# Seven block products instead of eight in the second MLP of a fused SSD, SwiGLU and softplus kernel

## The chip, the cores and the metric

The kernel runs on one core of a Trainium2 chip. The metric is the device time of one execution in microseconds (us), and what counts is the median of several executions. The profile is of one further execution on the same kind of core, and its times are counted from the start of its span. Engine names are those of the profile: PE is TensorE's matmuls, PEld its weight loads, DVE is VectorE, ACT is ScalarE, POOL is GpSimd, SP the engine that issues most DMAs.

## The reference

Three stages follow one another: a chunked state-space scan per head, a SwiGLU MLP, and an MLP with softplus. All is in fp32.

```python
# x: (4, 8, 768, 32); a: (4, 8, 768); B, C: (4, 8, 768, 16)
y = scan(x, a, B, C)                      # state carried along the 768 positions, per batch and head
x = y.transpose(0, 2, 1, 3).reshape(3072, 256)
xn = x / sqrt(mean(x * x, -1) + 1e-6) * rms_g
x = (silu(xn @ w_gate) * (xn @ w_val)) @ w_out        # layer 1: 256 -> 1536 -> 256
g = softplus(x @ w_in)                                # layer 2, first product: 256 -> 2048
return g @ w_out2                                     # layer 2, second product: 2048 -> 256
```

## The kernel before

The 3072 tokens are worked on as 24 units of 128 tokens (one batch, 128 positions). Four units make a tile of 512 tokens, so there are six tiles, 0 to 5. Tile t holds positions 128t to 128t+127 of all four batches, so the scan's state goes from each unit to the unit of the next tile with the same batch.

Both MLP layers keep features on the 128 partitions and 512 tokens along the free axis. Every product of two fp32 matrices is made of three fp32r matmuls: each operand is split into a high part and a rest, and high x high, rest x high and high x rest are added up in PSUM (`three_pass`, L834). One such matmul has a 128x128 weight and 512 columns.

- Layer 1 of a tile has 12 feature blocks f. `front1` (L857) makes gate and value of a block with 6 matmuls each into two banks of PSUM (tag `p`, 4 banks), ACT applies silu, DVE multiplies, `split_h` (L846) splits the result (ACT copies the high part, L396, DVE subtracts, L403) into a buffer `hw` (two of them). `back` (L891) multiplies it by `w_out` with 6 matmuls, adding to two banks of tag `t`. That is 18 matmuls a block, 216 a tile.
- Layer 2 of a tile has 16 blocks. `front2` (L877) makes 6 matmuls with `w_in` (names `wih`, `wil`), ACT applies softplus (L885), `split_h` splits, `back` makes 6 matmuls with the second weight (`wph`, `wpl`). That is 12 a block, 192 a tile, 96 of them in the first product.
- At the end of layer 1 the two `t` banks are split into `xxh` and `xxl`, the input of layer 2 (L927). At the end of layer 2 they are copied to buffers `s` (three of them, which softplus uses too) and sent to the output (L935).

The scan of a unit (`unit`, L533) needs two DVE scans (L604), two products with the decay (L653) and many small matmuls into banks of tag `a` (two). After four units, `norm` (L735) computes the RMS norm of the tile (L748 is its first operation on DVE for tiles 2 to 5, the split of the normalised input at L403 its last). `split` (L518) prepares B and C of a tile through buffers `wr` (three), through which the 34 chunks of weights come too (`weight`, L464).

What runs when is decided by a planner (`Plan`, L78 to L321) that writes out an order for every engine before the kernel is built. Each operation has a rank, a nominal time. The order of the layers is the list `seq` (L448 to L450): layer 1 of tiles 0 and 1, layer 2 of 0 and 1, then layer 1 and layer 2 of tile 2, of tile 3, then layer 1 of tiles 4 and 5, then layer 2 of 4 and 5. The planner starts an operation when its engine and its inputs are free, the lowest rank first; buffers of one tag are given out strictly in the order of the rank of their first operation (L189). The ranks of the scan (`base_of`, L511) and of `split` hang on the nominal start of layer 1 of their tile. Where layer 2 follows layer 1 of the same tile, two blocks of the next tile's layer 1 (`EARLY`) are put in between.

Of the kernel before, what the change touches and what calls it, by code (L numbers as in the profile page):

```python
# [17 lines left out]
P = 128  # L18
# [10 lines left out]

PAIRS = 2  # L30

EARLY, HEAD, TAIL = 2, 2, 2

FILL, SPARE = 200, 1e6

# [292 lines left out]
def tile_ssd_then_swiglu_then_softplus_mlp(  # L328
# [106 lines left out]
    W = {}  # L435
# [10 lines left out]
    blk_of = [i for i, b in enumerate(blocks) for _ in range(b["nu"])]  # L446

    seq = [(1, t) for t in range(HEAD)] + [(2, t) for t in range(HEAD)]  # L448
    seq += [(layer, t) for t in range(HEAD, len(blocks) - TAIL) for layer in (1, 2)]
    seq += [(layer, t) for layer in (1, 2) for t in range(len(blocks) - TAIL, len(blocks))]  # L450
    for layer, t in seq:
        b = blocks[t]
        b[f"t{layer}"] = t_nom
        t_nom += F1 * b["d1"] + b["nu"] * 1.4 if layer == 1 else F2 * b["d2"] + b["nu"] * 1.4


    chunks = []
# [385 lines left out]
    def wkeys(wt, f):  # L843
        return [(wt, f // 2, 0), (wt, f // 2, 1)]

    def split_h(key, s, n, rank, early=False):  # L846
        if early:
            hhl = buf("wr", [P, 8 * P + 64], I32, N_W)
            hhl.view = lambda t: t[:, 0:8 * P].bitcast(F32R).rearrange("p (s i) -> p s i", s=2)
        else:  # L850
            hhl = buf("hw", [P, 2, 4 * P], F32R, N_H)
        sv = lambda: s()[:, 0:n]
        COPY(n, rank - EPI, lambda: hhl()[:, 0, 0:n], sv, [s], [hhl])
        REST(n, rank - EPI, lambda: hhl()[:, 1, 0:n], sv, lambda: hhl()[:, 0, 0:n], [s, hhl], [(hhl, 1)], ("dve",))
        H[key] = hhl

    def front1(t, f, rank, new_table, early=False):  # L857
        bl = blocks[t]
        n = bl["n"]
        xh, xl = xnT[t]  # L860
        xk = xkeys[t]
        ps = []
        for wt in ("wg", "wv"):
            gp = pbuf("p", [P, 4 * P])
            PE(6 * n * MM * 1e3, rank, lambda gp=gp, wt=wt: three_pass(gp()[:, 0:n], wt, f, xh(), xl(), n),
               xk + wkeys(wt, f), [gp], 6 * n)
            ps.append(gp)
        s = buf("s", [P, 4 * P], F32, N_S)
        ACT(n, rank - EPI, lambda: act.activation(out=s()[:, 0:n], in_=ps[0]()[:, 0:n], func=ACTF.Silu), [ps[0]],  # L869
            [s, "table"] if new_table else [s], 1283 if new_table else 0)  # L870
        if not new_table:
            plan.readers.setdefault("table", []).append(len(plan.ops) - 1)
        DVE(n, rank - EPI, lambda: dve.tensor_tensor(out=s()[:, 0:n], in0=s()[:, 0:n], in1=ps[1]()[:, 0:n], op=ALU.mult),  # L873
            [s, ps[1]], [s], port=False)
        split_h((1, t, f), s, n, rank, early)

    def front2(t, f, rank, new_table):  # L877
        bl = blocks[t]
# [9 lines left out]
            plan.readers.setdefault("table", []).append(len(plan.ops) - 1)  # L888
        split_h((2, t, f), s, n, rank)

    def back(layer, t, f, rank):  # L891
        bl = blocks[t]
        n = bl["n"]
        nf, wt = ((F1, "wo"), (F2, "wp"))[layer - 1]
        if f == 0:
            acc[t] = [pbuf("t", [P, 4 * P]) for _ in range(KD)]
        hhl = H.pop((layer, t, f))

        end = (layer, t) == seq[-1] and f == nf - 1
# [12 lines left out]
        for m in range(0 if end else KD):  # L912
            def prod(m=m, o=acc[t][m]):
                a, b = (W[wt][s][:, f, m] for s in (0, 1))
                mm(o()[:, 0:n], a, swap(hhl()[:, 0, 0:n]), f == 0, False)
                mm(o()[:, 0:n], a, swap(hhl()[:, 1, 0:n]), False, False)
                mm(o()[:, 0:n], b, swap(hhl()[:, 0, 0:n]), False, f == nf - 1)
            PE(3 * n * MM * 1e3, rank, prod, [hhl, (hhl, 1)] + wkeys(wt, f), [acc[t][m]], 3 * n)
        if f < nf - 1:
            return  # L920
        if layer == 1:
            x2[t] = [buf(f"xx{k}", [P, KD, 4 * P], F32R, 3) for k in "hl"]
            for m in range(KD):
                h, l = ((lambda s=s, m=m: x2[t][s]()[:, m, 0:n]) for s in (0, 1))
                av = lambda a=acc[t][m]: a()[:, 0:n]
                COPY(n, rank - EPI, h, av, [acc[t][m]], [(x2[t][0], m)], False)
                DVE(n, rank - EPI, lambda h=h, l=l, av=av: dve.tensor_tensor(out=l(), in0=av(), in1=f32(h()), op=ALU.subtract),  # L927
                    [acc[t][m], (x2[t][0], m)], [(x2[t][1], m)], port=False)
        else:
            for m in range(KD):  # L930
                o = buf("s", [P, 4 * P], F32, N_S)
                COPY(n, rank - EPI, lambda o=o: o()[:, 0:n], lambda a=acc[t][m]: a()[:, 0:n], [acc[t][m]], [o], False,
                     ("dve",) if end and m else ("act",))
                c0 = bl["u0"] * P
                plan.op({"actq" if end and m else "sp": (1024, lambda o=o, m=m, q=act if end and m else nc.sync: q.dma_start(  # L935
                    out=out[m, :, c0:c0 + n], in_=o()[:, 0:n]))}, rank, [], [o])

    with tc.manual_schedule():
        plan.now = LOADS - 10
# [88 lines left out]
                steps = []  # L1028
        for c in range(len(chunks)):
            weight(c)  # L1030
        done = set()
        for j, (layer, t) in enumerate(seq):
            bl = blocks[t]
            if layer == 1:
                new = True
                for f in range(F1):
                    if (t, f) not in done:
                        front1(t, f, bl["t1"] + f * bl["d1"], new and j > 0 and seq[j - 1][0] == 2)
                        new = False
# [12 lines left out]


# [62 lines left out]
```

## Time and profile before

| | us |
|---|---|
| median of 3 executions (601.42 to 602.54) | 601.43 |
| the profiled execution | 600.79 |
| its span | 598.9 |
| PE busy | 593.7 (99%) |
| PEld busy | 513.3 (86%) |
| DVE busy | 351.3 (59%) |
| ACT busy | 310.0 (52%) |

The rows further down come from these views. The page's first part gives busy times, and its second the span in 40 slices. The view of waits says which engine stood idle for whom. The chain of work is followed back from the last instruction. The groups of instructions give how long one takes. The windows give the busy time of each engine in a stretch, and the timeline single instructions in order of time. The duration of a matmul in the profile overlaps that of the next: how fast matmuls follow one another is read from a run of them in the chain. Operations of DVE overlap in their records too.

### The profile page before, as it was taken

The page shows a single profiled execution, that of the slowest core. Times are in us where ns is not written, and L with a number is a line of the kernel's source. Part 1 is how long each engine was busy: PE and PEld are TensorE (multiplying, and loading weights), DVE is VectorE, ACT ScalarE, POOL GpSimd, SP SyncE. Part 2 cuts the span into 40 slices and gives each one's busy share as a digit, 9 for nine tenths or more (in the row PEclk, how much of TensorE's full clock was granted, in tenths as well). Part 3 has the DMA queues.
Part 4 walks back from the last instruction along what each step waited for, and adds up shares of the span by engine and source line. Part 5 has one row for each costly group of instructions (what it writes and reads, how often), then busy time and mean ns, then how long its engine had stood idle before and what let it go on. Part 6 is the DMA issues. An engine that isn't in the chain of part 4 may idle for free.

```text
span 598.9 us, 8785 instructions
## 1 busy us (share of the span) xinstructions
PE 593.7 (99%) x3385; PEld 513.3 (86%) x3385; DVE 351.3 (59%) x561; ACT 310.0 (52%) x547; POOL 19.7 (3%) x41
## 2 busy tenths in 40 slices
PE   9999999999999999999999999999999999999997
PEld 7888888888888888888888888888888888888886
DVE  6899978598876236694433779755333433322222
ACT  2676754678775445454555345655433333644543
POOL 3300000000000000000000000000000000000000
PEclk9999999999999999999999999999999999999999
DMA  6566648475661014111346433300000000000000
GB/s 213 189 223 210 217 150 273 120 240 220 240 169 58 0 50 172 49 54 31 134 172 205 149 128 93 115 1 0 36 1 1 1 1 1 0 1 0 36 1 36
DMA packets 33434, 59.76 MB, mean 100 GB/s; under 512 B 3120, under 2 KB 14960, under 8 KB 33392
## 3 DMA queue, kind: packets, MB, share of 16 engines
q1 hardware_dynamic: 33248, 58.93, 30.0%
q8 instruction: 27, 0.44, 0.3%
q10 hardware_dynamic: 144, 0.26, 0.1%
q14 instruction: 15, 0.12, 0.1%
HBM read 47.45 MB, written 11.73 MB: 99 GB/s over the span
## 4 chain that ended last, share of the span: by engine, by line
PE 97%; DVE 2%; issue 0%; DVEq 0%
PE p L360 55%; PE t L360 36%; PE a L360 6%; DVE ab L604 0%; DVE hw L403 0%; DVE s L873 0%; DVE xxh L767 0%; DVE xc L768 0%; DVE ab L653 0%; DVE xxl L821 0%; DVE s L397 0%; DVE xc L618 0%; DVE mean L988 0%; DVE small L989 0%; DVEq L873 0%
## 5 line engine op out<-in xcount | busy, mean ns | idle before, releaser
L403 DVE TENSOR_TENSOR hw<-s,hw 128x512 fp32r<-128x512 f32 x164 | 112.6, 688 | 135.9 <-ACT hw L396 83.5
L396 ACT ACTIVATE hw<-s 128x512 fp32r<-128x512 f32 x164 | 103.2, 631 | 110.6 <-DVE s L873 78.7
L360 PE MATMUL t<-hw,wph 128*128 128x512 f32 x384 | 114.6, 380 | 0.0
L885 ACT ACTIVATE s<-p 128x512 f32<-128x512 f32 x96 | 56.8, 596 | 73.9 <-PE p L360 71.9
L873 DVE TENSOR_TENSOR s<-s,p 128x512 f32<-128x512 f32 x72 | 49.2, 684 | 65.3 <-PE p L360 56.2
L360 PE MATMUL t<-hw,woh 128*128 128x512 f32 x272 | 81.5, 381 | 0.2 <-DVE hw L403 0.2
L360 PEld LDWEIGHTS t<-hw,wph 128*128 128x128 f32 x384 | 72.3, 189 | 10.5 <-issue 0.4
L360 PE MATMUL p<-xxh,wih 128*128 128x512 f32 x192 | 72.9, 380 | 0.0
L360 PE MATMUL p<-xxh,wil 128*128 128x512 f32 x192 | 72.8, 379 | 0.0
L360 PE MATMUL t<-hw,wpl 128*128 128x512 f32 x192 | 72.8, 379 | 0.0
L869 ACT ACTIVATE s<-p 128x512 f32<-128x512 f32 x72 | 42.8, 595 | 45.9 <-PE p L360 45.6
L360 PEld LDWEIGHTS t<-hw,woh 128*128 128x128 f32 x272 | 50.9, 189 | 8.1 <-DVE hw L403 0.6
L360 PE MATMUL p<-xxl,wih 128*128 128x512 f32 x192 | 57.1, 379 | 0.0
L360 PE MATMUL p<-xxh,wgh 128*128 128x512 f32 x144 | 55.1, 383 | 0.0
L360 PE MATMUL p<-xxh,wvh 128*128 128x512 f32 x144 | 55.0, 382 | 0.0
L360 PE MATMUL p<-xxh,wgl 128*128 128x512 f32 x144 | 54.7, 380 | 0.0
L360 PE MATMUL p<-xxh,wvl 128*128 128x512 f32 x144 | 54.6, 379 | 0.0
L360 PE MATMUL t<-hw,wol 128*128 128x512 f32 x136 | 51.5, 379 | 0.0
L604 DVE TENSOR_TENSOR_SCAN ab<-ab,ident 128x512 f32<-128x512 f32 x40 | 48.5, 1223 | 1.2 <-DMA ab<-a_clip 1.2
L360 PE MATMUL p<-xxl,wgh 128*128 128x512 f32 x144 | 42.8, 379 | 0.0
L360 PE MATMUL p<-xxl,wvh 128*128 128x512 f32 x144 | 42.8, 379 | 0.0
L360 PEld LDWEIGHTS p<-xxh,wih 128*128 128x128 f32 x192 | 36.3, 189 | 5.3 <-issue 0.2
(131 smaller groups left out, 751.5 us busy)
## 6 DMA issues: line engine op xcount, KB each, us to landing
wr<-in_w SPq DMA_DIRECT2D x34, 512.0 KB
ab<-a_clip SPq DMA_DIRECT2D x20, 512.0 KB
parts<-wr SPq DMA_DIRECT2D x16, 512.0 KB
xc<-in_xc SPq DMA_DIRECT2D x20, 256.0 KB
st<-parts SPq DMA_DIRECT2D x16, 256.0 KB
cz<-parts SPq DMA_DIRECT2D x32, 128.0 KB
out_y<-s SPq DMA_DIRECT2D x11, 256.0 KB
wr<-in_bc SPq DMA_DIRECT2D x8, 256.0 KB
```

The costliest lines, as they stand in the source:

```text
L360: pe.matmul(out=o, lhsT=l, rhs=r, start=start, stop=stop, skip_group_check=True)
L396: ways = {"act": (act_ns(n), lambda: act.activation(out=out(), in_=in_(), func=ACTF.Copy)), "dve": (dve_ns(n, sbuf), lambda: dve.tensor_co ...
L403: return lambda: eng.tensor_tensor(out=out(), in0=in_(), in1=f32(hi()), op=ALU.subtract)
L604: DVE(512, rank[0], lambda t=t, d=d: dve.tensor_tensor_scan(out=t(), data0=d(), data1=ident4, initial=0.0, op0=ALU.mult, op1=ALU.add), dk ...
L869: ACT(n, rank - EPI, lambda: act.activation(out=s()[:, 0:n], in_=ps[0]()[:, 0:n], func=ACTF.Silu), [ps[0]], [s, "table"] if new_table else ...
L873: DVE(n, rank - EPI, lambda: dve.tensor_tensor(out=s()[:, 0:n], in0=s()[:, 0:n], in1=ps[1]()[:, 0:n], op=ALU.mult), [s, ps[1]], [s], port= ...
L885: ACT(n, rank - EPI, lambda: act.activation(out=s()[:, 0:n], in_=hp()[:, 0:n], func=ACTF.Softplus), [hp], [s, "table"] if new_table and f ...
```

## The change

Layer 2's first product is done for two tiles and two blocks of features at once: tiles 2 and 3 are one pair, tiles 4 and 5 the other (`DUOS`). Written as 2x2 blocks (two halves of the 256 inputs, two blocks of features, two tiles), the product is four outputs of two block products each, eight block products in all, each of three matmuls. The change uses the Winograd form of Strassen's scheme with seven.

- The order of layers becomes: layer 1 of tiles 0 and 1, layer 2 of 0 and 1, layer 1 of 2, 3, 4 and 5, then the pair (2, 3), then the pair (4, 5).
- `operands` replaces the split at the end of layer 1 of tiles 2 to 5. It makes seven moving operands for a pair, each as a high part and a rest: three are the accumulators themselves, four are sums and differences, built on DVE.
- `sums` makes four sums of weight blocks for each of the 8 pairs of feature blocks, splits them and writes them over the weights of layer 1 (`wg`, `wv`), once, for both pairs of tiles.
- `duo` makes the seven products for a pair of tiles and a pair of feature blocks. They go to three banks `A`, `C` and `D`. The bank `A` is used by five of them in turn: what it holds is read (`snap`, a copy, or the softplus itself), and the next product is added to it. Three of the four outputs need an addition on DVE before their softplus (`plus`).
- The second product (`back`) stays as it was. The second tile of a pair adds into two banks of tag `a`.
- `EARLY` and its buffers go.

```diff
-EARLY, HEAD, TAIL = 2, 2, 2
+HEAD, DUOS = 2, [(2, 3), (4, 5)]
...
-    seq += [(layer, t) for t in range(HEAD, len(blocks) - TAIL) for layer in (1, 2)]
-    seq += [(layer, t) for layer in (1, 2) for t in range(len(blocks) - TAIL, len(blocks))]
+    seq += [(1, t) for t in range(HEAD, len(blocks))]
     for layer, t in seq:
         b = blocks[t]
         b[f"t{layer}"] = t_nom
         t_nom += F1 * b["d1"] + b["nu"] * 1.4 if layer == 1 else F2 * b["d2"] + b["nu"] * 1.4
+    duo_at, DUO = [], 45 * 4 * P * MM
+    for _ in DUOS:
+        duo_at.append(t_nom)
+        t_nom += F2 // 2 * DUO
...
+        if layer == 1 and t >= HEAD:
+            operands(t, rank - EPI)
...
+    def place(d, i):
+        wo = lambda k: ([lambda s=s: W["wo"][s][:, 2 * k:2 * k + 2].rearrange("p a k f -> p (a k f)") for s in (0, 1)],
+                        [("wo", k, 0), ("wo", k, 1)], [])
+        if i < 2 and d:
+            return halves(cz[i], lambda b: b.rearrange("p a z i -> p (a z i)")), [("cz", i, "h"), ("cz", i, "l")], [(("cz", i), z) for z in range(2)]
+        if d:
+            return wo(i - 2)
+        if i < 2 or i == 6:
+            b = buf("wr", [P, 8 * P + 64], I32, N_W)
+            return halves(b, lambda b: b()), [(b, "h"), (b, "l")], []
+        b = buf("xx" + "hl"[i % 2], [P, KD, 4 * P], F32R, 3)
...
+    def operands(t, rank):
+        d = [t in two for two in DUOS].index(True)
+        n = 4 * P
+        top = acc[t]
+        r = duo_at[d] - 45
+        def cut(i, x, xk, r, port):
+            (h, l), (hk, lk), more = place(d, i)
+            COPY(n, r, h, x, xk, [hk] + more, port)
+            DVE(n, r, lambda: dve.tensor_tensor(out=l(), in0=x(), in1=f32(h()), op=ALU.subtract), xk + [hk], [lk] + more, port=port)
+            B[d, i], Bk[d, i] = (h, l), [hk, lk]
+        def full(i, r, p, k):
+            COPY(n, r, lambda: zz[i], p, [k], [("zz", i)], False, ("act", "dve"))
+        if t == DUOS[d][0]:
+            for m in range(KD):
+                cut(m, lambda m=m: top[m](), [top[m]], rank, False)
+            if not d:
+                full(1, rank, lambda: top[0](), top[0])
+            return
+        full(0, rank, lambda: top[0](), top[0])
+        cut(6, lambda: top[1](), [top[1]], rank, False)
+        raw = [buf("ab", [P, 2, 4 * P], F32, N_AB) for _ in range(2)]
+        raw[0].rank, raw[1].rank = 1e5 + 2 * d, 1e5 + 2 * d + 1
+        T = [lambda i=i: raw[i // 2]()[:, i % 2] for i in range(4)]
+        tk = [(raw[i // 2], i % 2) for i in range(4)]
+        def mix(i, x, y, op, xk):
+            DVE(n, r, lambda: dve.tensor_tensor(out=T[i](), in0=x(), in1=y(), op=op), xk, [tk[i]])
+        b12, k12 = lambda: zz[0], [("zz", 0)]
+        def less(i, j, y, yk):
+            (h, l), (hk, lk) = B[d, j], Bk[d, j]
+            mix(i, lambda: f32(h()), y, ALU.subtract, yk + [hk])
+            mix(i, T[i], lambda: f32(l()), ALU.add, [tk[i], lk])
+        less(2, 6, b12, k12)
+        cut(4, T[2], [tk[2]], r, True)
+        if d:
+            (h, l), (hk, lk) = B[d, 0], Bk[d, 0]
+            mix(0, b12, lambda: f32(h()), ALU.subtract, k12 + [hk])
+            mix(0, T[0], lambda: f32(l()), ALU.subtract, [tk[0], lk])
+        else:
+            mix(0, b12, lambda: zz[1], ALU.subtract, k12 + [("zz", 1)])
+        less(1, 6, T[0], [tk[0]])
+        cut(3, T[1], [tk[1]], r, True)
+        less(3, 1, T[1], [tk[1]])
+        cut(5, T[3], [tk[3]], r, True)
+        cut(2, T[0], [tk[0]], r, True)
...
+    SUM = [("wg", i) for i in range(F1 // 2)] + [("wv", i) for i in range(F2 // 2 - F1 // 2)]
+    def sums(i, rank):
+        wt, at0 = SUM[i]
+        st = buf("st", [P, 4 * P], F32, 2)
+        q = lambda k: st()[:, k * P:(k + 1) * P]
+        hl = [lambda s=s: W["wi"][s][:, 2 * i:2 * i + 2].rearrange("p a k f -> p (a k f)") for s in (0, 1)]
+        to = [lambda s=s: W[wt][s][:, 2 * at0:2 * at0 + 2].rearrange("p a k f -> p (a k f)") for s in (0, 1)]
+        DVE(512, rank, lambda: dve.tensor_tensor(out=st(), in0=f32(hl[0]()), in1=f32(hl[1]()), op=ALU.add), wkeys("wi", 2 * i), [st])
+        def four():
+            for o, x, y, op in ((3, 2, 3, ALU.add), (2, 0, 2, ALU.subtract), (0, 3, 0, ALU.subtract), (1, 1, 0, ALU.subtract)):
+                dve.tensor_tensor(out=q(o), in0=q(x), in1=q(y), op=op)
+        DVE(512, rank, four, [st], [st], ns=4 * 200)
+        COPY(512, rank, to[0], st, [st], [(wt, at0, 0)])
+        REST(512, rank, to[1], st, to[0], [st, (wt, at0, 0)], [(wt, at0, 1)])
...
+    def duo(d, i, rank):
+        t, t9 = DUOS[d]
+        n = 4 * P
+        (wt, at0), q = SUM[i], DUO / 4
+        a_ = lambda k: [W["wi"][s][:, 2 * i + k // 2, k % 2] for s in (0, 1)]
+        s_ = lambda k: [W[wt][s][:, 2 * at0 + k // 2, k % 2] for s in (0, 1)]
+        wk, sk = wkeys("wi", 2 * i), wkeys(wt, 2 * at0)
+        A, C, D = (pbuf("p", [P, 4 * P]) for _ in range(3))
+        def three(o, w, b, start):
+            (wh, wl), (hi, lo) = w, B[d, b]
+            xh, xl = hi(), lo()
+            mm(o(), wh, swap(xh), start, False)
+            mm(o(), wl, swap(xh), False, False)
+            mm(o(), wh, swap(xl), False, True)
+        def PE3(r, o, w, b, wkey, start):
+            PE(3 * n * MM * 1e3, r, lambda: three(o, w(), b, start), Bk[d, b] + wkey, [o], 3 * n)
+        def plus(r, x, y, xk):
+            s = buf("s", [P, 4 * P], F32, N_S)
+            DVE(n, r - EPI, lambda: dve.tensor_tensor(out=s(), in0=x(), in1=y(), op=ALU.add), xk, [s], port=False)
+            return s
+        def soft(r, t, f, s, in_, rk):
+            new = not d and not i and (t, f) == (DUOS[0][0], 0)
+            ACT(n, r - EPI, lambda: act.activation(out=s(), in_=in_(), func=ACTF.Softplus), rk, [s, "table"] if new else [s], 1283 if new else 0)
+            if not new:
+                plan.readers.setdefault("table", []).append(len(plan.ops) - 1)
+            split_h((2, t, f), s, n, r)
+        f0, f1 = 2 * i, 2 * i + 1
+        def snap(r, p):
+            b = buf("st", [P, 4 * P], F32, 2) if p is D else buf("xc", [P, DM + 3 * P], F32, N_XC)
+            b.view = lambda x: x[:, 0:n]
+            COPY(n, r - EPI, b, p, [p], [b], False, ("act", "dve"))
+            return b
+        PE3(rank, A, lambda: a_(0), 0, wk, True)
+        PE3(rank + 0.01, C, lambda: a_(1), 1, wk, True)
+        c = snap(rank, A)
+        s = plus(rank, c, C, [c, C])
+        soft(rank, t, f0, s, s, [s])
+        PE3(rank + 0.02, D, lambda: s_(2), 4, sk, True)
+        d1 = snap(rank + 0.02, D)
+        PE3(rank + q, A, lambda: s_(0), 3, sk, False)
+        PE3(rank + q, D, lambda: a_(3), 5, wk, False)
+        c = snap(rank + q, A)
+        s = plus(rank + q, c, D, [c, D])
+        soft(rank + q, t, f1, s, s, [s])
+        PE3(rank + 2 * q, A, lambda: s_(3), 2, sk, False)
+        s = plus(rank + 2 * q, A, d1, [A, d1])
+        soft(rank + 2 * q, t9, f1, s, s, [s])
+        PE3(rank + 3 * q, A, lambda: s_(1), 6, sk, False)
+        s = buf("s", [P, 4 * P], F32, N_S)
+        soft(rank + 3 * q, t9, f0, s, A, [A])
+        back(2, t, f0, rank + 1.5 * q)
+        back(2, t, f1, rank + 2.5 * q)
+        back(2, t9, f1, rank + 3.5 * q, (1, F2 - 2), "a")
+        back(2, t9, f0, rank + 4.5 * q, (1, F2 - 2), "a")
...
-            if j + 1 < len(seq) and seq[j - 1] == (1, t) and j > 1:
-                t1 = seq[j + 1][1]
-                for f in range(EARLY):
-                    front1(t1, f, bl["t2"] - 0.1 + 0.01 * f, False, True)
-                    done.add((t1, f))
...
+        for d, two in enumerate(DUOS):
+            for i in range(F2 // 2):
+                if not d:
+                    sums(i, duo_at[0] + i * DUO - 60)
+                duo(d, i, duo_at[d] + i * DUO)
```

## Rows read from the trace of the kernel before

**Rows 1.** The page: busy time by engine, PE and its clock in 40 slices
```profile
PE 593.7 (99%) x3385; PEld 513.3 (86%) x3385; DVE 351.3 (59%) x561; ACT 310.0 (52%) x547; POOL 19.7 (3%) x41
...
PE   9999999999999999999999999999999999999997
...
PEclk9999999999999999999999999999999999999999
```

**Rows 2.** Waits of PE: engine line waited for, us in total, times, longest
```profile
PE p L360 <- DVE small L989: 0.9, 1, 0.9
PE t L360 <- DVE hw L403: 0.2, 1, 0.2
```

**Rows 3.** Chain of work, layers 1 and 2: start us, us, what, count of matmuls
```profile
444.56 2.59 PE p L360 x12
448.44 2.59 PE p L360 x12
...
510.60 2.59 PE p L360 x12
514.49 3.88 PE p L360 x18
518.37 2.59 PE t L360 x12
```

**Rows 4.** Groups of the page, layer 2's matmuls: count, busy us, mean ns, idle before
```profile
L360 PE MATMUL t<-hw,wph 128*128 128x512 f32 x384 | 114.6, 380 | 0.0
L360 PE MATMUL p<-xxh,wih 128*128 128x512 f32 x192 | 72.9, 380 | 0.0
L360 PE MATMUL p<-xxh,wil 128*128 128x512 f32 x192 | 72.8, 379 | 0.0
...
L360 PE MATMUL p<-xxl,wih 128*128 128x512 f32 x192 | 57.1, 379 | 0.0
```

**Rows 5.** Windows, layer 1 of tile 2 and with it tile 3's scan
```profile
core 0: us, PE busy (x) PEld busy (x) DVE busy (x) ACT busy (x) POOL busy (x), PEclk, DMA share, GB/s
222.50:274.70 52.20, 52.20 (x341) 45.12 (x340) 38.42 (x63) 23.20 (x42) 1.75 (x4) 1.00 0.28 92
```

**Rows 6.** Groups of the whole span used for the added operations
```profile
L873 DVE TENSOR_TENSOR s<-s,p 128x512 f32<-128x512 f32 x72 | 49.2, 684 | 65.3 <-PE p L360 56.2 <-ACT s L869 4.7 <-ACT zz L485 3.6
L618 DVE TENSOR_TENSOR xc<-xc 128x128 f32<-128x128 f32 x20 | 5.7, 283 | 0.0
L927 DVE TENSOR_TENSOR xxl<-t,xxh 128x512 fp32r<-128x512 f32 x12 | 8.0, 688 | 6.5 <-ACT xxh L396 6.5
L396 ACT ACTIVATE xxh<-t 128x512 fp32r<-128x512 f32 x12 | 7.1, 595 | 3.6 <-PE t L360 3.4
L885 ACT ACT_TABLE_LOAD x4 | 5.1, 1283 | 0.1
```

**Rows 7.** Groups of ACT and DVE in layer 2 of tiles 4 and 5, 518 to 592
```profile
L396 ACT ACTIVATE hw<-s 128x512 fp32r<-128x512 f32 x29 | 18.3, 631 | 6.9 <-PE t L360 5.6 <-DVE hw L403 0.7
L885 ACT ACTIVATE s<-p 128x512 f32<-128x512 f32 x28 | 16.6, 597 | 29.7 <-PE p L360 29.7
...
L403 DVE TENSOR_TENSOR hw<-s,hw 128x512 fp32r<-128x512 f32 x29 | 20.1, 693 | 54.5 <-PE t L360 33.4 <-ACT hw L396 21.1
```

**Rows 8.** Windows: layer 2 of tile 1, layer 1 of tile 5, layer 2 alone
```profile
181.00:222.50 41.50, 41.50 (x198) 36.46 (x197) 16.45 (x27) 21.59 (x36) 0.00 (x0) 1.00 0.11 34
463.80:513.00 49.20, 49.20 (x229) 43.09 (x228) 18.46 (x27) 17.94 (x29) 0.00 (x0) 1.00 0.00 1
518.00:592.00 74.00, 74.00 (x344) 64.82 (x343) 20.09 (x29) 35.60 (x59) 0.00 (x0) 1.00 0.02 8
```

**Rows 9.** Timeline: first scan products of tiles 3 and 4, their last splits
```profile
225.15 0.38 PE L360 MATMUL a<-xc,Sm 64*128 64x128 f32 x2
...
268.43 1.29 DVE L403 TENSOR_TENSOR xxl<-xxl,xxh 128x512 fp32r<-128x512 f32 x2
...
326.20 0.38 PE L360 MATMUL a<-xc,Sm 64*128 64x128 f32 x2
...
370.62 1.29 DVE L403 TENSOR_TENSOR xxl<-xxl,xxh 128x512 fp32r<-128x512 f32 x2
```

**Rows 10.** Timeline: the end of the kernel
```profile
591.58 0.60 ACT L885 ACTIVATE s<-p 128x512 f32<-128x512 f32 x1 [0.68 <-PE p L360]
...
592.27 0.63 ACT L396 ACTIVATE hw<-s 128x512 fp32r<-128x512 f32 x1
...
594.18 0.59 PE L360 MATMUL t<-hw,wph 128*128 128x512 f32 x2
594.60 0.60 ACT L396 ACTIVATE s<-t 128x512 f32<-128x512 f32 x1 [1.69 <-PE t L360]
...
595.22 0.33 SPq L935 DMA_DIRECT2D out_y<-s  x1
```

**Rows 11.** Last weights and tile 3's split; layer 2's second-last block; DMA
```profile
156.57 0.69 DVE L494 SCALAR_TENSOR_TENSOR wil<-wr,wih 128x512 fp32r<-128x512 f32 x1
...
158.82 0.69 DVE L525 TENSOR_TENSOR wr<-wr 128x512 fp32r<-128x512 f32 x1
159.43 0.69 DVE L494 SCALAR_TENSOR_TENSOR wpl<-wr,wph 128x512 fp32r<-128x512 f32 x1
...
173.61 0.38 PE L360 MATMUL p<-xxh,wih 128*128 128x512 f32 x1
...
177.50 0.38 PE L360 MATMUL t<-hw,wph 128*128 128x512 f32 x1
...
135.00:176.00 41.00, 41.00 (x248) 35.61 (x241) 33.71 (x56) 32.19 (x58) 1.07 (x3) 1.00 0.69 230
```

More of the change, by code (lines that the diff above doesn't have):

```diff
@@ L844, in wkeys, with split_h @@
         return [(wt, f // 2, 0), (wt, f // 2, 1)]
[L846 to L851, printed above, removed]
+    def split_h(key, s, n, rank):
+        hhl = buf("hw", [P, 2, 4 * P], F32R, N_H)
         sv = lambda: s()[:, 0:n]
@@ L855, in split_h, with front1 @@
         H[key] = hhl
-    def front1(t, f, rank, new_table, early=False):
+    def front1(t, f, rank, new_table):
         bl = blocks[t]
@@ L874, in front1 @@
             [s, ps[1]], [s], port=False)
-        split_h((1, t, f), s, n, rank, early)
+        split_h((1, t, f), s, n, rank)
     def front2(t, f, rank, new_table):
@@ L889, in front2, with back @@
         split_h((2, t, f), s, n, rank)
-    def back(layer, t, f, rank):
+    def back(layer, t, f, rank, order=None, tag="t"):
         bl = blocks[t]
@@ L894, in back @@
         nf, wt = ((F1, "wo"), (F2, "wp"))[layer - 1]
-        if f == 0:
-            acc[t] = [pbuf("t", [P, 4 * P]) for _ in range(KD)]
+        f0, f9 = order or (0, nf - 1)
+        if f == f0:
+            acc[t] = [pbuf(tag, [P, 4 * P]) for _ in range(KD)]
         hhl = H.pop((layer, t, f))
-        end = (layer, t) == seq[-1] and f == nf - 1
+        end = (layer, t) == (2, DUOS[-1][1]) and f == f9
         if end:
@@ L914, in prod @@
                 a, b = (W[wt][s][:, f, m] for s in (0, 1))
-                mm(o()[:, 0:n], a, swap(hhl()[:, 0, 0:n]), f == 0, False)
+                mm(o()[:, 0:n], a, swap(hhl()[:, 0, 0:n]), f == f0, False)
                 mm(o()[:, 0:n], a, swap(hhl()[:, 1, 0:n]), False, False)
-                mm(o()[:, 0:n], b, swap(hhl()[:, 0, 0:n]), False, f == nf - 1)
+                mm(o()[:, 0:n], b, swap(hhl()[:, 0, 0:n]), False, f == f9)
             PE(3 * n * MM * 1e3, rank, prod, [hhl, (hhl, 1)] + wkeys(wt, f), [acc[t][m]], 3 * n)
-        if f < nf - 1:
+        if f != f9:
             return
-        if layer == 1:
+        if layer == 1 and t >= HEAD:
+            operands(t, rank - EPI)
+        elif layer == 1:
             x2[t] = [buf(f"xx{k}", [P, KD, 4 * P], F32R, 3) for k in "hl"]
@@ L936, in back, with halves @@
                     out=out[m, :, c0:c0 + n], in_=o()[:, 0:n]))}, rank, [], [o])
+    B, Bk = {}, {}
+    def halves(b, view):
+        return [lambda k=k: view(b)[:, k * 4 * P:(k + 1) * 4 * P].bitcast(F32R) for k in range(2)]
+    def place(d, i):
[9 more added lines that the diff above has]
+        b = buf("xx" + "hl"[i % 2], [P, KD, 4 * P], F32R, 3)
+        b.rank = duo_at[0] - 20 + i // 2
+        return halves(b, lambda b: b().rearrange("p k i -> p (k i)")), [(b, "h"), (b, "l")], []
@@ L1030, in tile_ssd_then_swiglu_then_softplus_mlp @@
             weight(c)
-        done = set()
         for j, (layer, t) in enumerate(seq):
@@ L1036, in tile_ssd_then_swiglu_then_softplus_mlp @@
                 for f in range(F1):
-                    if (t, f) not in done:
-                        front1(t, f, bl["t1"] + f * bl["d1"], new and j > 0 and seq[j - 1][0] == 2)
-                        new = False
+                    front1(t, f, bl["t1"] + f * bl["d1"], new and j > 0 and seq[j - 1][0] == 2)
+                    new = False
                     back(1, t, f, bl["t1"] + (f + 0.5) * bl["d1"])
                 continue
-            if j + 1 < len(seq) and seq[j - 1] == (1, t) and j > 1:
-                t1 = seq[j + 1][1]
-                for f in range(EARLY):
-                    front1(t1, f, bl["t2"] - 0.1 + 0.01 * f, False, True)
-                    done.add((t1, f))
             for f in range(F2):
```

## The prediction

> **What bounds the kernel now.** I read the busy times first. PE is busy 593.7 of 598.9 us, in 39 of 40 slices at nine tenths or more and always at the full clock, while DVE and ACT stand at 59% and 52% [rows 1]. A busy PE need not be PE at its limit, so the waits come next: PE waited for others 1.1 us in all, 0.9 of it once at the start [rows 2]. Then the pace: in both layers twelve matmuls take 2.59 us and eighteen 3.88, so one follows another after 0.2158 us, though each is recorded with some 380 ns [rows 3, 4]. The end of the span is the same story: after PE's last matmuls come one copy and the output's DMA [rows 10]. So the kernel is bound by the number of 512-column matmuls from the first layer to 594 us. A matmul less is worth 0.2158 us, if nothing makes PE wait instead; and there is no idle time to win.
>
> **What is removed.** The first product of layer 2 has 6 matmuls per block and tile, so 24 for two blocks and two tiles; seven products of three are 21. Two pairs of tiles with 8 pairs of blocks each give 16 x 3 = 48 matmuls fewer (3385 to 3337), and 48 x 0.2158 = 10.4 us. The second product stays at 24. A pair of blocks (a duo, below) is then 45 matmuls, 9.71 us of PE.
>
> The row of the pace rules this term. The Trainium skill, TensorE: Matmul & The Clock Gate, Back-to-back issue gap, gives some 131 ns per 512-column matmul for a sustained stream of weight load and matmul, and 216 ns for one in isolation. By the 131 ns the 48 would be worth 6.3 us as an estimate, and the kernel would come out at 597; but the long streams of this trace run at the 216.
>
> **What is added beside PE, and does it fit.** A duo has four softplus (597 ns), four high copies (631 ns) and three snaps (by the nearest, the copy out of an accumulator, 595 ns): 6.7 us of ACT in 9.71, 69%, where layer 2 alone now has 35.6 in 74.0, 48%. DVE gets four rests (693 ns) and three additions from PSUM (684 ns): 4.8 us, 50%, now 27% [rows 6, 7, 8]. The weight sums cost DVE 0.69 + 4 x 0.283 + 0.69 = 2.5 us for each of 8 sets, 20 us. They overwrite layer 1's weights, so they can't start before tile 5 has used those, and by the strict turn of the `st` buffers the fourth waits for the first duo's snap. So five fall into the first pair's eight duos. The operands are 7 or 8 sums and differences and 7 rests of 0.69 us a pair, 10 us. The fullest stretch, the first pair, has on DVE 8 x 4.8 + 5 x 2.5 + 10.3 = 61 us in 78, 79%. Layer 1 of tile 2, with tile 3's scan beside it, has 38.4 in 52.2, 74%, and PE didn't idle there [rows 5]. I cost all this at nothing; what hides it is PE's own queue.
>
> **Waits inside a duo.** The trace has no bank that is read and added to again. Bank `A` goes through five products, and between them lie two snaps (0.6 us each) and one addition (0.68). Bounds: nothing, if PE has other matmuls, or all three in the open, 1.9 us a duo, 30 us. For cover PE has 24 second-product matmuls (5.2 us) and the other two banks in each duo, and a fourth `p` bank for the next duo's start. The two `hw` buffers turn over once per result: copy 0.63 and rest 0.69, 1.3 us, against 2.43 us from one second product's end to the start of the next but one's (9.71 / 4), now 2.59 and without a wait [rows 2, 7]. That row is the nearest, so I take 0.4 us for all sixteen, near nothing.
>
> **Start of the first duo.** From its first product to its first second product lie 0.65 + 0.60 + 0.68 + a table load 1.28 + 0.60 + 0.63 + 0.69 = 5.1 us [rows 6, 7]. Cover is layer 1's last 12 matmuls (2.6) and some 18 of the duos (3.9). Now the same turn runs without a gap, with 30 first-product matmuls ahead [rows 3]. Between 0 and 2.5 us (if the 2.6 alone cover); I take 0.4, and 0.2 for the change of pairs.
>
> **The end.** `s` buffers are given out by rank, and the two copies of tile 4's output (rank of its last `back` less EPI, 2.5 quarters into the duo) stand ahead of the last softplus (3 quarters). So after tile 4's last matmul ACT does two copies, a softplus and a high copy, 0.60 + 0.60 + 0.60 + 0.63 = 2.4 us, before tile 5's last six matmuls may start; six others (1.3 us) cover. PE waits 1.1 us. Now softplus and high copy come in time and PE doesn't stop [rows 10]. Bounds 0 and 2.0 (tile 5's second output may also wait for a buffer whose DMA is still out: from issue to the end of the span it takes 598.9 - 595.2 = 3.7 us).
>
> **The scan moves.** Tile 3's normalised input is needed where it is now, tile 4's some 50 us sooner, tile 5's sooner too. Now tile 3 takes from its first product to its last split 44.6 us (225.15 to 269.7) and tile 4 45.7 [rows 9]. The new order has one such tile beside each of three layer-1 stages, and layer 1 of tile 2 is already just that: 52.2 us, PE never idle [rows 5]. The stages get 2 to 3 us of DVE more for the operands. So 0, with 7 us of slack in each stage. The removed `EARLY` blocks covered a turn from layer 1 to layer 2 of the same tile that no longer exists: 0, no gain since PE had no gap there. Nor can the other moves win more than a few tenths.
>
> **Sum.** -10.4 + 0.4 + 0.4 + 0.2 + 1.1 = -8.3. Profiled: 600.8 - 8.3 = 592.5. The profiled execution was 0.64 below the median, so the median becomes 601.4 - 8.3, 593.2 rounded up. Own range 591.0 (no wait anywhere) to 595.5 (start 2.5, end 2.0, duos 0.4).
>
> **Rivals.**
> - Duos that wait (0.17). ACT at 69% and DVE at 79% work strictly in order, and a snap behind a copy lets bank `A` wait. At 0.3 us a duo, half of one snap, that is 4.8 us: 598; range 595.5 to 600. At 8.3 / 16 = 0.52 us a duo the gain is gone. For it: the first pair's load; against it: 5.2 us of cover a duo.
> - The scan comes late (0.08), and the kernel gets slower. Place: the norm of tiles 4 and 5, whose chain on DVE and ACT runs beside layer 1's results. It decides above 52.2 us per tile, and eats the gain at 52.2 + 8.3 / 3 = 55 us. At 57 us PE idles 3 x 4.8 = 14.4 us: 607. For it: the three slots of `xxh`/`xxl` allow no two tiles ahead, and DVE has some 41 of 52 us. Against: 45 us now, and in layer 2 of tile 1 DVE works only 16.45 of 41.5 us, where tile 3 can begin [rows 8].
> - Late weights (0.05). Tile 3's nominal start falls from 348 to 301, so its `split` gets rank 136, ahead of the last three weight chunks (138 to 143), where it came after them. That is 2.6 MB, 11.4 us at the 230 GB/s of that stretch. Margins are 16 us (156.6 + 0.7 to 173.6) and 17 us (160.1 to 177.5) [rows 11]. Twice the delay costs 4 to 7 us: 597.
> - The clock (0.02). All 40 slices have the full 2.4 GHz, though PE changes banks every 3 to 18 matmuls [rows 1, 3]. Small gaps in the duos could drop it; each microsecond of PE work at 1.2 GHz costs one more, and 8.3 of the duos' 155 us eat the gain. That it can: the Trainium skill, TensorE: Matmul & The Clock Gate, A second HAM failure mode, tells of a kernel that cycled PSUM banks with micro-idles and swung between both clocks. By that rule this would land at 601 or above; the trace shows none of it so far.
> - The change doesn't do what it says (0.03): as many matmuls as before, 601.4.
>
> **How the numbers follow.** Forecast 0.65, 593.2. A measurement of this kernel tells 0.2%, 1.2 us, from no change. Faster by more than that, below 600.2: 0.65 + 0.16 of the duos + 0.05 of the weights + 0.01 of the scan = 0.87. Within it, 600.2 to 602.6: 0.03 + 0.01 + 0.01 = 0.05. Slower: 0.06 of the scan + 0.02 of the clock = 0.08. The range 591 to 600 holds forecast, duos and weights, some 0.85.
>
> **What would show it.** 3337 PE matmuls, and the pace still 0.2158. PE's waits: a few tenths each for the first duo, and about 1 us at the end on the last `hw` or `s`. If waits of PE on `st`, `xc` or `s` in the duos sum up to several us, the duo term is wrong; if PE waits on `xxh` or `xxl` before layer 1 of tiles 4 or 5, the scan's; if on weights before 180 us, the third rival's. PE busy falling by much less than 10 us with no waits would mean a slower pace or a lower clock.

## The result, and the profile after

| | before | with the change |
|---|---|---|
| median, us (4 executions each) | 601.57 | 592.03 (591.36 to 592.58) |
| ratio to before, 95% interval | | 0.9838 (0.982 to 0.9855) |
| profiled execution / its span, us | 600.79 / 598.9 | 592.1 / 590.3 |
| PE busy, us; matmuls | 593.7; 3385 | 584.9; 3337 |
| DVE busy / ACT busy, us | 351.3 / 310.0 | 414.3 / 334.4 |

The change gains 9.5 us, 1.6%. A second measurement of it gave 591.67 and 0.9835 (0.9822 to 0.9849). It lies between the 593.2 of the forecast and the 591.0 that no wait at all would have given.

The page after, its first two parts (compare [rows 1]):

```profile
PE 584.9 (99%) x3337; PEld 504.6 (85%) x3337; DVE 414.3 (70%) x683; ACT 334.4 (57%) x603; POOL 20.1 (3%) x41
...
PE   9999999999999999999999999999999999999997
...
DVE  6899989588879478687977773464399754555453
ACT  2667655578686546435534433443377765767574
...
PEclk9999999999999999999999999999999999999999
```

There are 48 matmuls fewer. DVE and ACT have more to do, above all in the last third. PE is as full as before, and the granted clock is at the 2.4 GHz level throughout. The waits of PE after (as [rows 2]: line waited for, us in total, times, longest):

```profile
PE p L360 <- DVE small L1140: 0.9, 1, 0.9
PE a L360 <- ACT hw L396: 0.3, 1, 0.3
```

The first is the wait at the start that was there before. The second is new, and one place: the end. The view counts only gaps behind the recorded end of a matmul, which lies some 160 ns past the start of the next. For the smaller ones I added up the distances between the starts of neighbouring matmuls of the two layers and took 0.2158 us off for each ("over the pace" below): 2.48 us in the whole span before, 3.50 after. So 1.0 us of waiting more stands against 10.36 us removed. It is made of 0.7 us in the duos and 0.8 at the end, less a wait of 0.46 us that the kernel before had where layer 1 of tile 3 ends, and that is gone (before):

```profile
370.76 0.48 PE L360 MATMUL t<-hw,woh 128*128 128x512 f32 x1 [0.20 <-DVE hw L403]
```

The rest of the account is the start. Layer 1's first matmul starts at 29.82 us in this profile and at 29.12 in that of before, behind the same work. In twelve profiled executions of the kernels told of here, which all begin alike, it lies between 29.1 and 30.4, and in a second profile of the change at 29.45. The difference arises in the first 6 us, where PE's first matmuls start 0.43 us apart before they start 0.22 apart: some seven in the profile before, ten in that after (the column of the granted clock reads 1.00 there all the same). It varies from one execution of the same kernel to the next, so it is chance, and -10.36 + 1.0 + 0.7 = -8.6 is the difference of the two spans, 598.9 to 590.3. The medians have less of that luck in them: they differ by 9.5, near the 9.3 that matmuls and waits give.

Windows after (us from:to, length, busy and count of PE, PEld, DVE, ACT, POOL, the granted clock, DMA share, GB/s): layer 1 of tile 2, layer 1 of tile 3, then the duos of the first and of the second pair (compare [rows 5, 8]):

```profile
229.00:282.00 53.00, 53.00 (x345) 45.86 (x345) 43.08 (x72) 24.75 (x44) 1.75 (x4) 1.00 0.37 115
282.00:334.00 52.00, 52.00 (x313) 44.99 (x312) 40.82 (x69) 22.80 (x44) 0.87 (x2) 1.00 0.19 60
...
432.00:507.00 75.00, 74.89 (x346) 64.71 (x345) 53.47 (x96) 53.60 (x96) 0.00 (x0) 1.00 0.00 1
507.00:584.00 77.00, 77.00 (x358) 67.07 (x356) 39.08 (x58) 51.96 (x92) 0.00 (x0) 1.00 0.04 16
```

In the first pair ACT and DVE are at 71% each, in the second ACT at 67%; by this view PE is idle for 0.1 us in the first pair's window and never in the second's.

Early in the first pair the duos run behind DVE. The chain of work after, 434.86 to 443.31 (start us, us, what), and PE's timeline where that chain ends:

```profile
434.86 1.20 DVE s L1050 x2
436.06 0.60 DVE wgl L403
436.66 1.20 DVE ab L989 x2
437.87 0.60 DVE hw L403
...
443.31 1.35 PE a L360 x5
```

```profile
442.83 0.97 PE L360 MATMUL a<-hw,wph 128*128 128x512 f32 x2
```

Additions (L1050), the rest of a weight sum (`wgl`), two sums of operands for the second pair (L989) and a rest (L403) stand in one queue of DVE, each 0.60 us after the other. All that comes of it is one pair of matmuls whose second starts 0.48 us after the first instead of 0.22.

The end, ACT's and PE's timeline after (compare [rows 10]):

```profile
582.17 1.25 ACT L396 ACTIVATE s<-t 128x512 f32<-128x512 f32 x2
583.31 0.59 ACT L1055 ACTIVATE s<-p 128x512 f32<-128x512 f32 x1
583.94 0.63 ACT L396 ACTIVATE hw<-s 128x512 fp32r<-128x512 f32 x1
```

```profile
582.40 0.38 PE L360 MATMUL t<-hw,wpl 128*128 128x512 f32 x1
582.62 0.85 PE L360 MATMUL a<-hw,wph 128*128 128x512 f32 x2
...
583.95 0.38 PE L360 MATMUL a<-hw,wpl 128*128 128x512 f32 x1
584.62 0.48 PE L360 MATMUL a<-hw,wph 128*128 128x512 f32 x1 [0.29 <-ACT hw L396]
```

The two output copies of tile 4 come ahead of the last softplus and its high copy, six matmuls cover, and PE starts the last six 0.67 us after the matmul before instead of 0.22. With 0.1 us right behind that, and 0.25 us at the result before (582.6 to 583.3), the end loses 0.8 us.

### The profile page after: what moved, and what is told of

It is laid out like the page before. It is cut to its first block, busy times and chain, and to the rows that moved or that the text cites. A ratio compares the mean times of both kernels' runs of the same rounds, so it can differ in the third digit from the quotient of the medians.

```text
span 590.3 us, 8851 instructions
## 1 busy us (share of the span) xinstructions
PE 584.9 (99%) x3337; PEld 504.6 (85%) x3337; DVE 414.3 (70%) x683; ACT 334.4 (57%) x603; POOL 20.1 (3%) x41
## 4 chain that ended last, share of the span: by engine, by line
PE 97%; DVE 2%; ACT 0%; issue 0%
PE p L360 53%; PE t L360 30%; PE a L360 13%; DVE hw L403 0%; DVE st L1023 0%; DVE s L1050 0%; DVE ab L989 0%; DVE wol L970 0%; DVE st L1019 0%; DVE s L397 0%; DVE st L397 0%; ACT hw L396 0%; DVE zz L397 0%; DVE wgl L403 0%; ACT s L396 0%
## 5 line engine op out<-in xcount | busy, mean ns | idle before, releaser
L403 DVE TENSOR_TENSOR hw<-s,hw 128x512 fp32r<-128x512 f32 x168 | 115.4, 687 | 53.5 <-ACT hw L396 52.3
L360 PE MATMUL t<-hw,wph 128*128 128x512 f32 x256 | 76.5, 380 | 0.0
L868 ACT ACTIVATE s<-p 128x512 f32<-128x512 f32 x72 | 42.9, 595 | 55.6 <-PE p L360 55.4
L360 PE MATMUL p<-xxh,wgh 128*128 128x512 f32 x168 | 64.0, 382 | 0.0
L360 PEld LDWEIGHTS t<-hw,wph 128*128 128x128 f32 x256 | 47.7, 189 | 7.0 <-issue 0.6
L360 PE MATMUL t<-hw,wpl 128*128 128x512 f32 x128 | 48.5, 379 | 0.0
L1055 ACT ACTIVATE s<-s 128x512 f32<-128x512 f32 x48 | 30.0, 625 | 25.8 <-DVE s L1050 25.6
L360 PE MATMUL a<-hw,wph 128*128 128x512 f32 x128 | 39.1, 382 | 0.4 <-ACT hw L396 0.3
L360 PEld LDWEIGHTS p<-xxh,wgh 128*128 128x128 f32 x168 | 31.7, 189 | 4.8 <-issue 0.4
L1050 DVE TENSOR_TENSOR s<-xc,p 128x512 f32<-128x512 f32 x32 | 22.0, 686 | 16.9 <-PE p L360 11.9
L360 PEld LDWEIGHTS p<-xxl,wgh 128*128 128x128 f32 x156 | 29.5, 189 | 4.3 <-ACT xc L396 0.2
```

The costliest lines, as they stand in the source:

```text
L360: pe.matmul(out=o, lhsT=l, rhs=r, start=start, stop=stop, skip_group_check=True)
L403: return lambda: eng.tensor_tensor(out=out(), in0=in_(), in1=f32(hi()), op=ALU.subtract)
L1050: DVE(n, r - EPI, lambda: dve.tensor_tensor(out=s(), in0=x(), in1=y(), op=ALU.add), xk, [s], port=False)
L1055: ACT(n, r - EPI, lambda: act.activation(out=s(), in_=in_(), func=ACTF.Softplus), rk, [s, "table"] if new else [s], 1283 if new else 0)
```

## The experiments

The theory: the time follows the number of matmuls at 0.2158 us, and all else lies under PE's queue. The rivals: the new order or the pairing moves the time by itself; DVE or ACT bound the duos; the scan has little slack.

**Seven products, one of them twice.** Everything of the change stays, but PE has as many matmuls as before.

```diff
-        PE3(rank + 0.01, C, lambda: a_(1), 1, wk, True)
+        twice(rank + 0.01, C, lambda: a_(1), 1, wk)      # three(...) two times, start=True both
```

> Each duo's product into bank C is made twice, so 48 matmuls a duo instead of 45 and 3385 in all, as in the kernel before; order, operands, sums and snaps stay those of the change. If the gain is the number of matmuls alone: 592.0 + 48 x 0.2158 = 602.4, less at most 0.4 us where the extra matmuls fill waits of PE, so 602.0 to 602.4 (the kernel before: 601.6). Rival, that the new order or the pairing itself gains or costs: a time off that by what it brings, below 600 or above 604.

Measured: 602.77 us, 1.0021 of before (1.0012 to 1.0031). The 48 matmuls are worth 602.77 - 592.03 = 10.7 us, 11.0 by the two ratios, so the whole gain is theirs; order and pairing together bring nothing, and with all they add cost 1.3 us. Its matmuls stand 3.88 us over the pace, 1.4 more than before the change, which is that. It is also 0.4 more than after the change, so the matmuls themselves are worth 10.4 of the 10.7 us, and the time came out 0.4 us above the 602.0 to 602.4 that I expected: the extra matmuls filled no waits. (The planner's nominal length of a duo goes from 45 to 48 matmuls with this edit, and to 38 in the run with two passes; those lines are not shown.)

**Only the order.** The kernel before, without duos.

```diff
-    seq += [(layer, t) for t in range(HEAD, len(blocks) - TAIL) for layer in (1, 2)]
-    seq += [(layer, t) for layer in (1, 2) for t in range(len(blocks) - TAIL, len(blocks))]
+    seq += [(layer, t + i) for t in (2, 4) for layer in (1, 2) for i in range(2)]
```

> The kernel before with its order changed alone: layer 1 of two tiles, then layer 2 of the two, for the pairs (2, 3) and (4, 5) as for (0, 1); no duos, 3385 matmuls. If order and an earlier scan are free: 601.6, within 1 us. Rival, that an order with fewer turns between the layers saves time by itself: 599 or less. Rival, that the scan of tiles 3 to 5 comes late: 604 or more, with PE waiting on xxh or xxl.

Measured: 602.0 us, 1.0013 (1.0003 to 1.0023), at most 1.4 us of cost and no gain. PE waits for nobody after the start: the 0.46 us at 370 are gone here too (2.02 us over the pace instead of 2.48), too little to show in the times. It has the scan of tile 3 one layer of 41 us earlier than before; those of tiles 4 and 5 it leaves where they were, so the scan as early as the change wants it is not tried by this run.

**Two of three passes in the duos.** This leaves part of the product out, for a shorter PE stretch over the same work of ACT and DVE.

```diff
             mm(o(), wh, swap(xh), start, False)
-            mm(o(), wl, swap(xh), False, False)
-            mm(o(), wh, swap(xl), False, True)
+            mm(o(), wl, swap(xh), False, True)
```

> Leaves out the third pass (high weight times the rest of the operand) of the seven products in the duos, so 38 matmuls a duo instead of 45, 112 fewer in all; ACT and DVE do the same work. If PE bounds the duos with room to spare: 592.0 - 112 x 0.2158 = 592.0 - 24.2 = 567.8. Rival, that DVE and ACT are near their limit in the duos: the first pair has 53.5 us of DVE work in 75 of PE, now in 64; a duo has 8.2 us of PE for 6.7 of ACT, and waits on hw, s and the snaps give back 4 us or more, 572 to 580. I expect 569 to 571, most of the waits in the first pair.

Measured: 570.98 us, 21.1 less than the change where 112 matmuls are worth 24.2. The 3.1 us stand over the pace in its profile (6.65 against 3.50), and most of them in the first duos, where PE waits for the addition ahead of a softplus:

```profile
PE p L360 <- DVE s L1049: 1.4, 2, 1.2
```

So the duos still have room at 45 matmuls, and at 38 the start of the first pair meets DVE.

**All snaps on DVE.**

```diff
-            COPY(n, r - EPI, b, p, [p], [b], False, ("act", "dve"))
+            COPY(n, r - EPI, b, p, [p], [b], False, ("dve",))
```

> The changed kernel with all 48 snaps on DVE, where 44 of them ran on ACT. DVE had 53.5 us in the 75 us of the first pair; 22 more of 0.69 make 68.7 by records, and it would be full through the first duos, which already ran behind DVE (the chain of work goes over DVE from 430.7 to 443.3). If DVE is the next bound in the first pair: PE waits of 3 to 8 us there, 595 to 600, and none in the second pair (39.1 us in 77). Rival, that PE's queue hides this too: 592.

Measured: 592.82 us, 0.9862 (0.9845 to 0.9878), 0.8 us above the change by the medians and 1.4 by the ratios, where I expected three at least if DVE bound. Its matmuls stand 4.19 us over the pace, 0.7 more. The window of the first pair:

```profile
432.00:507.00 75.00, 74.93 (x343) 63.95 (x342) 64.65 (x115) 42.85 (x73) 0.00 (x0) 1.00 0.01 2
```

DVE is at 86% there and PE is full. I had reckoned with records of 0.69 us; an operation of DVE takes 0.60 of its queue, as the chain above shows, so there was room. The rival, that PE's queue hides this too, came true but for that microsecond.

**One pair alone.** Tiles 4 and 5 by seven products, tiles 2 and 3 as before.

```diff
-HEAD, DUOS = 2, [(2, 3), (4, 5)]
+EARLY, HEAD, DUOS = 2, 2, [(4, 5)]
...
-    seq += [(1, t) for t in range(HEAD, len(blocks))]
+    seq += [(layer, t) for t in (2, 3) for layer in (1, 2)] + [(1, 4), (1, 5)]
```

> The pair of tiles 4 and 5 alone by seven products; tiles 2 and 3 as in the kernel before, with the two early blocks of layer 1. If each pair gains by its 24 matmuls: 601.6 - 5.2 + 0.5 (half of the waits found after the change) = 596.9. Rival, that the gain comes from layer 1 of tiles 2 to 5 in a row: 600 to 602.

Measured: 606.71 us, slower than before: 1.0088 (1.0073 to 1.0104), and 10 us off what I expected. The wait of PE, the windows of that place and the chain of work through it:

```profile
PE p L360 <- ACT xxh L396: 5.7, 1, 5.7
```

```profile
514.50:520.50 6.00, 0.35 (x3) 0.08 (x1) 3.98 (x7) 4.45 (x8) 0.00 (x0) 0.79 0.00 0
520.50:525.00 4.50, 4.50 (x11) 3.19 (x12) 4.43 (x9) 2.12 (x4) 0.00 (x0) 0.52 0.00 0
```

```profile
513.47 0.66 PE t L360 x3
...
514.16 0.60 ACT zz L396
...
514.77 1.28 ACT L1059
...
517.21 0.69 DVE wr L974
517.90 2.40 DVE ab L993 x4
520.31 1.20 DVE xxh L974 x2
```

Layer 1 of tile 5 starts its last matmul at 514.4. Only as its two banks are done can they be copied (`zz`) and, behind a table load and a softplus on ACT, be cut (`wr`), the four differences be built (L993) and the next operand be split (`xxh`). PE has no other work and stands from 514.6 to 520.4. The granted clock falls to half: 0.52, the 1.2 GHz level, in the 4.5 us in which PE works again. Idle PE (5.8 us), half clock (2.3 us) and shorter waits, for the rest of the operands and elsewhere, make up the loss: 12.87 us over the pace, 10.4 more than before, less the 5.2 that 24 matmuls are worth, is the 5.3 us by which the medians differ.

**The same pair with work in front.** Layer 2 of tile 3 moves behind layer 1 of tile 5.

```diff
-    seq += [(layer, t) for t in (2, 3) for layer in (1, 2)] + [(1, 4), (1, 5)]
+    seq += [(1, 2), (2, 2), (1, 3), (1, 4), (1, 5), (2, 3)]
```

> As the one-pair run, but layer 2 of tile 3 moved behind layer 1 of tiles 4 and 5, so that 41 us of PE work lie between the end of layer 1 of tile 5 and the pair (4, 5). If the loss of the one-pair run was the operands' chain standing open after layer 1 of tile 5 (6.0 us of idle PE) and the half clock after it: PE waits there are gone and the time is 601.6 - 5.2 + 0.5 to 1.5 = 597 to 598. Rival, that one pair alone is slow for another reason (the duos, the sums): 602 or more.

Measured: 596.58 us, 0.9921 (0.9906 to 0.9935). The wait is gone, and one pair gains 4.7 us by the ratio, for 24 matmuls worth 5.2, a little more than I expected. So the open chain was the loss, and the order of the change is what hides it: between layer 1 of tile 3 and the first pair lie 94 us of layer 1 of tiles 4 and 5, and the second pair has the first one in front.

**A longer norm.** Ten Newton steps in the norm of tiles 2 to 5 instead of three; an even number turns the sign of what the layers get.

```diff
-            for _ in range(3):
+            for _ in range(10):
```

> The changed kernel with 10 Newton steps in the norm of tiles 2 to 5 instead of 3: each tile's chain is longer by 7 x (0.63 + 0.69 + 0.69) = 14.1 us, with 9.6 us more of DVE and 4.4 of ACT. By the prediction's reckoning a tile has 7 us of slack beside its layer-1 stage: then three stages lose up to 7 us each, 600 to 613. By the profile after, the last split of tile 4 ends at 291.9 and its layer 1 starts at 334.6, tile 5's at 335.4 and 381.2, so the slack is over 40 us and only DVE (43.1 of 53 us in the stage of tile 2) can bind: 592 to 593.

Measured: 604.77 us, 12.7 more than the change, and not the 592 to 593 that I read off the profile after. It lies in the 600 to 613 that I had by the prediction's reckoning. The change's timeline, last splits of tiles 4 and 5 beside the first matmuls of their layer 1, and the same place for tile 4 with the long norm:

```profile
290.56 0.69 DVE L403 TENSOR_TENSOR xxl<-xxl,xxh 128x512 fp32r<-128x512 f32 x1
...
334.19 1.28 DVE L403 TENSOR_TENSOR xxl<-xxl,xxh 128x512 fp32r<-128x512 f32 x2
...
334.61 0.38 PE L360 MATMUL p<-xxh,wgh 128*128 128x512 f32 x1
...
381.23 0.38 PE L360 MATMUL p<-xxh,wgh 128*128 128x512 f32 x1
```

```profile
336.04 1.30 DVE L403 TENSOR_TENSOR xxl<-xxl,xxh 128x512 fp32r<-128x512 f32 x2
```

```profile
332.36 0.38 PE L360 MATMUL t<-hw,wol 128*128 128x512 f32 x1
336.06 0.80 PE L360 MATMUL p<-xxh,wgh 128*128 128x512 f32 x1 [3.32 <-ACT xxh L396]
```

In the change tile 4 is ready 43 us ahead (291.2 to 334.6) and tile 5 46. That is a lead, not slack per tile: the tiles go one behind the other. From one tile's last splits to the next one's it takes 45 to 57 us in the change (they start at 182.7, 240.2, 289.4 and 334.2 for tiles 2 to 5), and with the long norm 57 to 67 (203.3, 268.7, 336.0 and 392.9), against stages of 47 to 53 us. Two steps at that rate use the lead up: tile 3 still comes 10 us early, PE waits 3.3 us for tile 4's, and behind it matmuls start 0.43 us apart for a while, at a granted clock of 0.50 (336.0 to 338.5). This is the rival of the late scan as the prediction told it: it decides where a tile takes longer than a stage. Not all of the 12.7 us is that wait; the profile has 13.8 us over the pace, 10.3 more than the change, spread over waits in layer 1 of tiles 3 to 5, the half clock behind the longest of them, the duos and the end. The rest lies outside this count, 0.6 us of it in the start.

**The end and the sums.** Tile 4's two output copies get their buffers after the last softplus, and one of them goes to DVE. The weight sums get a rank 70 instead of 60 ahead of their duo.

```diff
+                late = t == DUOS[-1][0]
+                if late:
+                    o.rank = rank - EPI + 2
...
-                     ("dve",) if end and m else ("act",))
+                     ("dve",) if (end or late) and m else ("act",))
...
-                    sums(i, duo_at[0] + i * DUO - 60)
+                    sums(i, duo_at[0] + i * DUO - 70)
```

> The changed kernel with two edits. The output copies of tile 4 get their buffer behind the last softplus, and one of the two goes to DVE; the weight sums get rank 70 instead of 60 ahead of their duo, so that four sets instead of three are made before the first duo. If the waits at the end (0.15 + 0.45 us) came from the copies ahead of the softplus, and those of the first duos (0.4 us) from DVE: 0.5 to 0.9 us less than the changed kernel, a span of 589.5 or so beside its 590.3, 591.3 us. Rival, that the last wait is that for the hw buffer: no change.

> The kernel with the edits at the end and in the sums once more: its profile had 0.8 us less waiting between matmuls than the changed kernel (2.67 against 3.50 us over the pace), so 591.2 beside 592.0; no difference if the runs' spread of 0.6 us hides it.

> The changed kernel once more, beside the next run on the same chip: 592.0, ratio to the kernel before 0.984. By the sum of matmuls removed (10.36 us) less the waits found in its profile (1.0 us of matmul pace over the kernel before) 9.3 us less than the kernel before.

Measured: 591.63 us, 0.9836 (0.9821 to 0.9851); again 591.29, 0.9827 (0.9814 to 0.9841), beside the change with 591.67 and 0.9835 (0.9822 to 0.9849). By the times it can't be told from the change, though both medians lie 0.4 us lower, a little less than I expected. The profiles are clearer: 2.67 and 2.70 us over the pace instead of 3.50, and ACT's timeline at the end has the softplus ahead of the copy:

```profile
581.68 0.60 ACT L1058 ACTIVATE s<-p 128x512 f32<-128x512 f32 x1
582.33 0.60 ACT L396 ACTIVATE s<-t 128x512 f32<-128x512 f32 x1
583.04 0.63 ACT L396 ACTIVATE hw<-s 128x512 fp32r<-128x512 f32 x1
```

The waits at the end are gone, so they came from the copies and the order of work that hangs on them (the planner also moved three matmuls of PE there). The one at 442.8 in the first duos stayed (0.48 us between two matmuls). That does not clear the sums of it: the fourth set was made earlier (397.2), but another still begins just ahead of that place, at 440.35 where the change has one at 440.19:

```profile
440.35 0.69 DVE L1022 TENSOR_TENSOR st<-wih,wil 128x512 f32<-128x512 f32 x1
```

Its cause, beyond the full queue of DVE, stays open.

## Why the prediction was right

**The bound and the removed matmuls.** Both right. 48 fewer, and 10.7 us by the run that puts them back, 10.36 by the term. The pace held at 0.2158 us. The 131 ns for a sustained stream in the Trainium skill, TensorE: Matmul & The Clock Gate, Back-to-back issue gap, and the estimate of 6.3 us from it, did not come out of this trace.

**ACT and DVE beside PE.** DVE was reckoned at 79% in the first pair and stood at 71%: records overlap, and an operation takes 0.60 us of the queue. ACT was reckoned at 69% in a duo and stood at 71 and 67%, but that agreement is luck. The reckoning left out the high copies of the weight sums and of the operands, which ACT made too (`wgh`, `wvh`, `woh`; ten in the first pair's window), and it added up records, which overlap on ACT as well: the records that start in that window add up to 58.3 us, 78%. Three of them in a row start 0.52 us apart:

```profile
436.51 0.62 ACT L396 ACTIVATE hw<-s 128x512 fp32r<-128x512 f32 x1
437.03 0.62 ACT L1055 ACTIVATE s<-s 128x512 f32<-128x512 f32 x1
437.55 0.59 ACT L1055 ACTIVATE s<-p 128x512 f32<-128x512 f32 x1
```

Costing all this at nothing was right, and the snaps on DVE show that it would be, but for a microsecond, with DVE at 86%.

**Waits in the duos, the start, the change of pairs.** 1.0 us was taken together. Found: 0.7, of it 0.4 at 442.8, 0.2 at 460 and some 0.1 at 434 and 438, and nothing between the pairs.

**The end.** The mechanism was right, the size was not: 1.1 us taken for the wait ahead of the last six matmuls, 0.55 found, and 0.25 more at the result before, which the prediction did not have. The step that was mis-sized is the 2.4 us of ACT after tile 4's last matmul. It does take 2.4 us (582.17 to 584.57), but the first copy starts before that matmul, when the first of the two banks is done: 582.17 against 582.40. In the run with the copies behind the softplus the waits are gone.

**The sum.** -8.3 forecast, -8.7 in the profiled execution and -9.5 by the medians. The waits were taken at 2.1 us and are 1.5, and 0.46 came back that the prediction put at nothing: it says that PE had no gap at the turns that `EARLY` covered, and [rows 2] has one, 0.2 us on `hw`, which is the wait at 370. It is gone in the change and in the run of the order alone. These two are 1.0 of the 1.2 us by which the medians gained more than forecast. The profile of before had an early start of layer 1, which the prediction carried along as a constant offset of 0.64 us; part of the offset was chance.

**The scan.** 0 was right. The 7 us of slack in each stage was the right kind of number, a rate. The lead of 40 us on top, which comes from tile 3 starting in layer 2 of tile 1, was only a remark among the rivals.

**What the prediction missed without harm.** It said that PE's queue hides the operands. The one-pair run shows that a queue of a few matmuls does not: the chain is 6 us and more, and 94 us of layer 1 hide it. The change works because of its order, though the order gains next to nothing itself.

**The weights.** The rival had the last chunks 11.4 us later, and the last two came 13 us later (compare [rows 11]; DVE's timeline after):

```profile
169.62 0.69 DVE L497 SCALAR_TENSOR_TENSOR wil<-wr,wih 128x512 fp32r<-128x512 f32 x1
...
172.84 0.68 DVE L497 SCALAR_TENSOR_TENSOR wpl<-wr,wph 128x512 fp32r<-128x512 f32 x1
```

Layer 2's second-last block uses them at 176.1 and 181.3, so 6 and 8 us were left, and it cost nothing.

**The clock.** PE changes banks every 3 to 12 matmuls in the duos, with starts up to 0.48 us apart there and 0.67 at the end, and the granted clock stayed at 2.4 GHz. The Trainium skill, TensorE: Matmul & The Clock Gate, A second HAM failure mode, tells of a kernel whose clock swung with short idle times between groups of matmuls; the trace of the change does not show that for gaps of this size. Where PE started nothing for 5.8 us, in the one-pair run, and for 3.7 us with the long norm, the granted clock did fall to the 1.2 GHz level.

## What to carry to other kernels

Where one engine is full from end to end, an algorithm that does less on it pays by its own count, if each new wait has other work of that engine in front: ask of every new chain what the full engine does meanwhile, and price the chain in the open. A change of order that gains next to nothing by itself can be what makes another change pay, and taking the parts one by one then misleads. A lead that the profile shows is not slack: compare how long a link of the chain takes with how long its stage gives it.

## What was not expected of the hardware

In a queue of DVE 128x512 fp32 operations start 0.60 us apart, though each is recorded with 0.68 to 0.69; on ACT they start some 0.52 us apart, recorded with 0.58 to 0.63. After 5.8 us without work, PE's matmuls ran at a granted clock of 0.52 for 4.5 us: nine of them started 0.43 to 0.59 us apart, which added 2.3 us to the wait. A softplus from SBUF took 625 ns and one from PSUM 588:

```profile
L1055 ACT ACTIVATE s<-s 128x512 f32<-128x512 f32 x48 | 30.0, 625 | 25.8 <-DVE s L1050 25.6
...
L1055 ACT ACTIVATE s<-p 128x512 f32<-128x512 f32 x16 | 9.4, 588 | 0.6 <-PE p L360 0.6
```
